# Attention feeding an MLP on one core: the last 64 tokens of every batch move to the final chunk, and the opening is re-ordered

## The chip, the cores and the metric

One core of a Trainium2 chip. The metric is device microseconds of one execution, taken as the median of the runs. One execution was also profiled, and its trace carries all line numbers (L...) used here. They are lines of the kernel before, unless the text says "of the changed kernel".

## The reference

Linear attention over 8 batches, 8 heads, 576 tokens and 64 dimensions, then an MLP with tanh shrinkage over the 4608 tokens:

```
phi(x) = where(x > 0, x, exp(x) - 1) + 1
kv  = einsum('bhsd,bhse->bhde', phi(k), v);   z = sum_s phi(k)
num = einsum('bhsd,bhde->bhse', phi(q), kv);  den = einsum('bhsd,bhd->bhs', phi(q), z) + 1e-6
x   = (num / den), transposed to (4608 tokens, 512)
h   = x @ w_in (512x2048);  g = h - tanh(h);  out = g @ w_out (2048x512)
```

q, k, v and the weights come in fp32; the loads turn them into bf16.

## The kernel before

**Tiling.** The 576 tokens of a batch are split as (64 positions p, 9 steps j), token 9p + j. `xT` (128, 4 pairs of heads, 4608 tokens) is the MLP's input, transposed; the MLP runs over NC = 9 chunks of 512 columns of `xT`. In a chunk, the first layer is 64 matmuls of 512 columns (`l1mm`, L434; in chunk 0 the first four blocks are L701 with 256 columns), then tanh on ScalarE (L440, L445) and the subtraction on VectorE (L441, L446) into `gT`; the second layer is 64 matmuls of 512 columns (`l2mm`, L455), an eviction to `osb` (L466) and stores (L479). Columns of `xT` lie batch after batch, 576 each, so chunk c needs batch c and the end of batch c - 1.

**Attention beside it.** The work of batch c + 1 and c + 2 is hung into the loops of chunk c: `s1[fi]` holds what is issued after block fi of the first layer, `s2[s]` what is issued after step s of the second. The order of every engine's instructions is the order in which the program issues them (manual schedule). Each engine works its own list in order and waits on semaphores.

**Names.** `phi_pieces` (L125) makes exp on ScalarE, max/add and min on VectorE. `a_qT_pe` (L161) transposes phi(q) on TensorE, nine blocks for each of two values of i, and copies them out of PSUM. `kv_mm` (L179) multiplies phi(k) by v, 72 matmuls of 64x64. For batch 0 it is `b0_kv` (64 columns), with the sums z apart in `b0_z` (L253). For batch 1 it is `a_kv`, whose right side is v next to a block of ones: 128 columns. For the others it is `kv_cols_mm`, with a packed copy `vp` of v that holds two columns of ones: 66 columns. `num_mm` (L274) makes the numerator of steps j = 0 to 7 (512 tokens), `rest_mm` (L282) that of j = 8 (64 tokens: "the rest"). `a_den` (L340) makes the denominators, L350 their reciprocal. In batches 0 and 1 the reciprocals of the first 512 tokens are spread over the partitions by TensorE (L303, L423) and those of the rest by a round trip through DRAM (`spread_rest`, L316 and L319), and the rest is scaled by `scale_rest` (L327).

**PSUM.** `ps_all` is 8 banks of 512 fp32 columns. The chunk loops use banks 0 to 5, the attention work of chunk 1 onward banks 6 and 7, besides banks 0 to 3 for the numerators (`a_num`, L378). `a_num` of the last batch (b = 7), issued in chunk 6, ends with copies of the numerators (banks 0 to 3) and of the rest (bank 6 by VectorE, bank 7 by ScalarE) into `xT`.

**Opening.** q, k and v of batch 0 arrive by GpSimd's DMA queue, then w_in, and behind a gate (`load_rest`) the other weights and batch 1. Dummy matmuls (`spin`, L542) fill TensorE's waits. The order on TensorE is: z of i = 0, z of i = 1, kv of i = 0, denominators, numerators, kv of i = 1, spread, L701.

Of the kernel before, what the change touches and what calls it, by code (L numbers as in the profile page):

```python
# [18 lines left out]
def kernel(  # L19
# [9 lines left out]
    nc = tc.nc  # L29
# [46 lines left out]
    kz_c = [const.tile([128, 2, 2, 96], BF16, name=f"kz{i}") for i in range(2)]  # L76

    v_b = [const.tile([128, 3, 2, J, D], BF16, name=f"v{i}") for i in range(2)]
# [4 lines left out]

    def load(b, t, src, halves):

        x = src[b].rearrange("h (p j) d -> (h p) (j d)", j=J)
        if halves:
            y = x.rearrange("(h i q) x -> i q h x", h=2, i=2)
            for i in range(2):
                for hs in ((0, 1), (1, 2)) if i and src is k and b == 0 else ((0, 2),):  # L90
                    nc.gpsimd.dma_start(out=t[:, hs[0]:hs[1], i].rearrange("q h j d -> q h (j d)"),
                                        in_=y[i, :, hs[0]:hs[1]])
        else:
            nc.gpsimd.dma_start(out=t.rearrange("q h i j d -> q (h i) (j d)"),  # L94
                                in_=x.rearrange("(n q) x -> q n x", n=4))
# [9 lines left out]
    def load_v(b):  # L105
        load(b, v_b[b % 2][:, 0:2], v, b < 2)
# [11 lines left out]
    def load_wo2(n):  # L118
        nc.gpsimd.dma_start(out=w_out_sb[:, 8 + 2 * n:10 + 2 * n, :],
                            in_=moe_w_out[1024 + 256 * n:1280 + 256 * n, :].rearrange("(ko ki) f -> ki ko f", ki=128))  # L120
# [4 lines left out]
    def phi_pieces(b, src, store, name, i, parts=0):  # L125
# [3 lines left out]
        x = src[b][:, :, i]  # L129
        e = epool.tile([128, 2, J, D], BF16, name="e")  # L130
        r = r_t[b] = epool.tile([128, 2, J, D], BF16, name="r")
        y = store[b][:, i].rearrange("p j h d -> p h j d")
        if parts:

            return ([lambda h=h: nc.scalar.activation(e[:, h], x[:, h], AF.Exp) for h in range(2)],  # L135
                    lambda: nc.vector.tensor_scalar(r, x, 0.0, 1.0, ALU.max, ALU.add),
                    [lambda h=h: nc.vector.tensor_tensor(y[:, h], e[:, h], r[:, h], ALU.min) for h in range(2)])
# [23 lines left out]
    def a_qT_pe(b, i, banks, on="AV"):  # L161
# [3 lines left out]
        for n in range(2):  # L165
            j0, j1 = ((0, 5), (5, 9))[n]
# [21 lines left out]
    def a_kv(b, b0):  # L188

        kz_t[b], vt = kz_c[b % 2], v_b[b % 2]  # L190
        kv_mm(b, lambda rs, h, i, j: vt[rs, h:3:2 - h, i, j, :],
              lambda cs, hg, i: ps_all[cs, b0 + hg, 128 * i:128 * i + 128].rearrange("p (a e) -> p a e", a=2))

    def a_kz(b, b0):
        ps = ps_all[:, b0:b0 + 2, 0:256].rearrange("p g (i e) -> p g i e", i=2)
        nc.vector.tensor_mul(kz_t[b][:, :, :, 64:96], ps[:, :, :, 64:96], mask)
        nc.vector.tensor_copy(kz_t[b][:, :, :, 0:64], ps[:, :, :, 0:64])

    def a_vp(b, i, eng=nc.vector):
        eng.tensor_copy(vp[:, i, :, :, 0:64].rearrange("p j h d -> p h j d"), v_b[b % 2][:, 0:2, i])  # L200

    def kv_cols_mm(b, b0, o):
        kz_t[b] = kz_c[b % 2]
        kv_mm(b, lambda rs, h, i, j: vp[rs, i, j, h, :],
              lambda cs, hg, i: ps_all[cs, b0 + hg, o + 66 * i:o + 66 * i + 66])
# [44 lines left out]
    def b0_z(i):  # L250

        for j in range(J):
            nc.tensor.matmul(ps_all[:, 5 - 3 * i, 0:2], kp_t[0][:, i, j].rearrange("p h d -> p (h d)"), two,  # L253
                             start=(j == 0), stop=(j == J - 1))

    def b0_zc(i):
        nc.vector.tensor_mul(kz_t[0][:, :, i, 64:96],
                             ps_all[:, 5 - 3 * i, 0:2].unsqueeze(2).to_broadcast([128, 2, 32]), mask[:, :, i, :])
# [18 lines left out]
    def rest_mm(b, b0, o):  # L277

        kz, qT = kz_t[b], qT_t[b]
        for i in range(2):  # L280
            for rs, cs, h, hg in quads():
                nc.tensor.matmul(ps_all[cs, b0 + h, 64 * i + o:64 * i + o + 64], kz[rs, hg, i, 0:64],  # L282
                                 qT[rs, i, 8, hg, :], start=True, stop=True)
# [28 lines left out]
    def spread_rest(b):  # L312

        ds = dram.tile([H, 4, 16], F32, name="ds0")
        for t in range(4):
            nc.sync.dma_start(out=ds[:, t, :], in_=rden_t[b][32 * t:32 * t + H, 128:144])  # L316
        rdb = rpool.tile([128, NP, 4, 16], F32, name="rdb0")
        for hh in range(2):
            nc.sync.dma_start(  # L319
                out=rdb[64 * hh:64 * hh + 64].rearrange("p a t c -> p (a t c)"),  # L320
                in_=ds[4 * hh:4 * hh + 4].rearrange("h t c -> (h t c)").partition_broadcast(64))
        rdb_t[b] = rdb

    def scale_rest(b, pss):
        rdb = rdb_t[b]
        for h, ps in enumerate(pss):
            nc.vector.tensor_mul(  # L327
                xT[:, 2 * h:2 * h + 2, S * b + 512:S * b + 576].rearrange("p a (t c) -> p a t c", t=4),
                ps.rearrange("p a (t c) -> p a t c", t=4), rdb[:, 2 * h:2 * h + 2])

    def a_den(b, bank, parts=range(4)):

        kz, qT = kz_t[b], qT_t[b]
        ps = ps_all[:, bank, 0:J * 16]
        for t in range(4) if b == 0 else ():
            nc.tensor.matmul(ps[32 * t:32 * t + 32], eps[:, 0:32], one[:, 0:J * 16], start=True, stop=False)
        for n, p in enumerate((0, 2, 1, 3)):
            if n in parts:
                for t in range(4):
                    nc.tensor.matmul(ps[32 * t:32 * t + 32], kz[:, p // 2, p % 2, 64:96],  # L340
                                     qT[:, p % 2, :, p // 2, 16 * t:16 * t + 16],
                                     start=(n == 0 and b > 0), stop=(n == NP - 1))
        if b > 0:
            den = rpool.tile([128, J * 16], F32, name="den")
# [3 lines left out]
        rden = rpool.tile([128, J * 16], F32, name="rden")  # L348
        for x in (slice(0, 128), slice(128, 144)) if b == 0 else (slice(0, 144),):
            nc.vector.reciprocal(rden[:, x], den[:, x])  # L350
        rden_t[b] = rden

    def a_split(b):

        f = rden_t[b]
        t1 = rpool.tile([128, J * 16], BF16, name="t1")
        u = rpool.tile([128, J * 16], F32, name="u")
        t2 = rpool.tile([128, J * 16], BF16, name="t2")
        w = rpool.tile([128, J * 16], BF16, name="w")
# [18 lines left out]
    def a_num(b, nxt):  # L378
# [8 lines left out]
        if b == B - 1:  # L387
            t = S * b + 448
            for h, copy in enumerate((nc.vector.tensor_copy, nc.scalar.copy)):
                two = slice(2 * h, 2 * h + 2)  # L390
                copy(xT[:, two, S * b:t], ps_all[:, two, 0:448])
                copy(xT[:, two, t:t + 128:2], ps_all[:, two, 448:512])
                copy(xT[:, two, t + 1:t + 128:2], rest[h])
        elif b >= QS:
            for h, copy in enumerate((nc.vector.tensor_copy, nc.scalar.copy)):
                copy(xT[:, 2 * h:2 * h + 2, S * b:S * b + 512], ps_all[:, 2 * h:2 * h + 2, :])
                copy(xT[:, 2 * h:2 * h + 2, S * b + 512:S * b + 576], rest[h])
# [3 lines left out]
    def num_scale(b, rest):  # L401

        rdb = rdb_t[b]
        for n in range(NP):
            nc.vector.tensor_mul(
                xT[:, n, S * b:S * b + 512].rearrange("p (j t c) -> p j t c", j=8, t=4),
                ps_all[:, n, :].rearrange("p (j t c) -> p j t c", j=8, t=4),
                rdb[:, n, :, 0:8, :].rearrange("p t j c -> p j t c"))
        for h in range(2):
            nc.vector.tensor_mul(  # L410
                xT[:, 2 * h:2 * h + 2, S * b + 512:S * b + 576].rearrange("p a (t c) -> p a t c", t=4),
# [14 lines left out]
    def a_scale(b, p, ns, n):  # L426
        nc.vector.tensor_mul(
            xT[:, p, S * b:S * b + 512].rearrange("p (j t c) -> p t j c", j=8, t=4),
# [31 lines left out]
    def evac(c, i, o, f0=0, f1=None):  # L460
# [7 lines left out]
        if c == NC - 1 and i == 3:  # L468
            nc.sync.dma_start(
                out=out[(B - 1) * S:, f0:f1].rearrange("(p j) m -> p j m", j=J)[:, J - 2:J],  # L470
# [3 lines left out]
        def store():  # L474
            for half in range(2):
                b, j = divmod(2 * (4 * c + i) + half, J)
                cuts = [f0, 256, f1] if c == 3 else [f0, f1]
# [21 lines left out]
    def load_rest(r):  # L499
        nc.gpsimd.tensor_copy(rpool.tile([1, 1], BF16, name="g0"), r[0:1, 1, J - 1, 63:64])  # L500
# [6 lines left out]
        load_wo2(0)  # L507
        nc.gpsimd.memset(v_b[1][:, 2], 1.0)
        nc.gpsimd.memset(vp[:, :, :, :, 64:66], 1.0)
        load_v(1)  # L510
        load_wo2(1)
        load_wo(3)
# [36 lines left out]
    spin(18)  # L549
    t0a, t0v = a_qT_pe(0, 0, side, "AA")  # L550
    t0a()
    (ek0, rk0, mk0), (ek1, rk1, mk1) = (phi_pieces(0, k_t, kp_t, "kp", i, 2 * i) for i in range(2))
    for f in (ek0, rk0):
        f()
    spin(4)
    t1a, t1v = a_qT_pe(0, 1, side)
    for f in (*ek1, t0v, t1a, mk0, rk1, *mk1):
        f()
    load_rest(r_t[0])
    spin(6)  # L560
# [4 lines left out]
    b0_z(1)  # L565
    b0_kv(0)
    b0_kz(0)
    b0_zc(1)
    a_den(0, 4)
# [5 lines left out]
    spread_rest(0)  # L575
# [21 lines left out]

    for c in range(NC):
# [4 lines left out]
        if c == 0:  # L603
# [7 lines left out]
            def kv1():  # L611
                a_kv(1, 4)
                pss = rest_mm(0, 4, 256)
                a_kz(1, 4)
                scale_rest(0, pss)
# [11 lines left out]
            s2[5].append(lambda: ([f() for i in range(2) for f in a_qT_pe(1, i, Banks([4 + 2 * i, 5 + 2 * i]))], a_kphi(1, 1),  # L627
# [3 lines left out]
            s2[10].append(lambda: (a_den(1, 4), num1(), spread_rest(1), a_split(1)))  # L631
# [16 lines left out]
            s2[13].append(lambda: exp2(qs, q_t, qp_t, "qp", 0))  # L648
            s2[14].append(lambda: exp2(qs, q_t, qp_t, "qp", 1))
            s2[15].append(lambda: (rest2(qs[0]), rest2(qs[1]), a_qT_dma(2), [f() for f in later], k2(0), k2(1)))  # L650
        elif n1 < B:
            if c == 1:
                def kv2():
                    kv_cols_mm(2, 6, 0)
                    pss = rest_mm(1, 6, 256)
                    kz_copy(2, 6, 0)
                    scale_rest(1, pss)
# [12 lines left out]
            s2[m].append(lambda: a_num(n1, n2 if n2 < B else 0))  # L670
            if n2 < B:
                s2[m + 2].append(lambda: (q_zb(n2, 4 if c == 1 else 7), q_prod(n2)))
                if c > 1:
                    s2[15].append(lambda: (q_den(n2, 0, 0), q_den(n2, 0, 1)))
        if c == 1:
# [53 lines left out]
        for s in range(16):  # L729
# [14 lines left out]
            if c == 0 and g == 2:  # L744
                for n in (2 * i, 2 * i + 1):
                    f = 8 + 2 * (n // 4)
# [37 lines left out]
```

## Time and profile before

| what | value |
|---|---|
| median of 3 runs | 284.19 us (284.14 to 284.21) |
| the profiled execution | 284.06 us |
| its span (first to last instruction) | 282.3 us |
| granted TensorE clock | 0.999 |
| TensorE busy | 274.2 us, 97% of the span |
| start of the first MLP matmul (L701) | 16.19 us |
| first 512-column matmul of the MLP (L434) | 20.01 us |
| last eviction (L464) | 279.15 us |

The span is what the trace covers; 1.8 us of the execution lie outside it. A duration of a matmul in the trace is its latency (379 ns for 512 columns), while matmuls that follow each other start about 216 ns apart (47 of them take 10.31 us in the chain of waits); so distances between starts are read, not durations.

### The profile page before, as it was taken

Reading aid. Unit: us, or ns where it says so; the run is one execution under the profiler, and the core shown is the slowest. Engines: PE = TensorE matmul, PEld = TensorE weight load, DVE = VectorE, ACT = ScalarE, POOL = GpSimd, SP = SyncE. Lnnn points to the kernel's source line nnn. Section 1 sums busy time; section 2 is a strip of 40 time slices with the busy share of each in tenths; the row PEclk is TensorE's granted clock in tenths of the full one; section 3 lists DMA queues with packets and bytes.
Section 4 is the critical chain, followed back from the end, with each engine's and each line's share of the span. In section 5 each row is a group of like instructions: output and inputs, shape, how many; then the busy total and the mean of one; then the engine's idle time right before and its main releaser. Section 6 shows DMA issues by size and latency. Waiting matters only on the chain.

```text
span 282.3 us, 5058 instructions
## 1 busy us (share of the span) xinstructions
PE 274.2 (97%) x2052; PEld 131.6 (47%) x2082; DVE 175.0 (62%) x281; ACT 145.9 (52%) x176; POOL 78.2 (28%) x71
## 2 busy tenths in 40 slices
PE   8899999999999999999999999999999999999995
PEld 3574464444444454445444544454444444444443
DVE  5759967994879764978397639764870167006600
ACT  3747648846356753566366735572651365126411
POOL 8663120330361526233614360506050000000000
PEclk9999999999999999999999999999999999999999
DMA  6999999899993399049903792252115210230032
GB/s 105 201 204 213 206 206 208 159 189 225 236 237 67 76 190 205 17 84 160 228 17 77 115 237 60 51 107 52 25 25 123 57 29 2 59 80 11 2 74 75
DMA packets 38759, 33.12 MB, mean 117 GB/s; under 512 B 16176, under 2 KB 34640, under 8 KB 38608
## 3 DMA queue, kind: packets, MB, share of 16 engines
q0 software_dynamic: 17520, 18.35, 40.2%
q1 hardware_dynamic: 21216, 14.45, 21.7%
q8 instruction: 16, 0.26, 0.3%
q14 instruction: 7, 0.06, 0.1%
HBM read 38.14 MB, written 9.46 MB: 169 GB/s over the span
## 4 chain that ended last, share of the span: by engine, by line
PE 90%; DMA 4%; ACT 2%; issue 2%; DVE 1%; SPq 0%; POOL 0%; DVEq 0%; POOLq 0%
PE ps_all L434 43%; PE ps_all L455 40%; DMA out_dram<-osb 2%; PE ps_all L185 2%; DMA qraw<-in_q_dram 2%; PE ps_all L701 1%; PE ps_all L274 1%; ACT osb L466 1%; ACT e L138 1%; SPq L479 0%; ACT e L135 0%; PE ps_all L303 0%; PE ps_all L340 0%; DVE rden L350 0%; ACT qT L173 0%
## 5 line engine op out<-in xcount | busy, mean ns | idle before, releaser
L455 PE MATMUL ps_all<-w_out_sb,gT 128*128 128x512 bf16 x542 | 122.6, 379 | 1.6 <-issue 1.0
L434 PE MATMUL ps_all<-xT,w_in_sb 128*128 128x512 bf16 x549 | 121.9, 379 | 0.7 <-issue 0.2
L441 DVE TENSOR_TENSOR gT<-ps_all,th 128x1024 bf16<-128x1024 f32 x64 | 77.8, 1218 | 45.9 <-ACT th L440 45.9
L440 ACT ACTIVATE th<-ps_all 128x1024 f32<-128x1024 f32 x64 | 65.5, 1023 | 47.4 <-PE ps_all L434 46.7
L434 PEld LDWEIGHTS <-w_in_sb 128*128 128x128 bf16 x560 | 54.7, 98 | 65.6 <-issue 0.3
L455 PEld LDWEIGHTS <-gT 128*128 128x128 bf16 x560 | 53.8, 98 | 63.1 <-issue 0.2
L466 ACT COPY osb<-ps_all 128x512 f32<-128x512 f32 (+1 forms) x36 | 20.9, 582 | 57.0 <-PE ps_all L455 39.3
L246 POOL TENSOR_TENSOR qp<-qp,rd 128x1152 bf16<-128x1152 bf16 x10 | 21.0, 2118 | 39.1 <-issue 23.7
L232 POOL TENSOR_TENSOR pr<-qp,zb 128x1152 f32<-128x1152 bf16 x10 | 23.4, 2360 | 21.0 <-ACT zb L225 18.5
L237 DVE TENSOR_REDUCE dn<-pr 128x9 f32<-128x576 f32 x20 | 14.5, 745 | 12.2 <-POOL pr L232 12.2
L138 ACT ACTIVATE e<-qraw 128x1152 bf16<-128x1152 bf16 x16 | 18.5, 1161 | 3.5 <-DMA qraw<-in_q_dram 3.5
L138 ACT ACTIVATE e<-kraw 128x1152 bf16<-128x1152 bf16 x15 | 17.4, 1162 | 2.1 <-DMA kraw<-in_k_dram 2.1
L140 DVE TENSOR_TENSOR qp<-e,r 128x1152 bf16<-128x1152 bf16 x16 | 12.1, 758 | 4.6 <-ACT e L138 3.6
L140 DVE TENSOR_TENSOR kp<-e,r 128x1152 bf16<-128x1152 bf16 x15 | 11.4, 757 | 5.0 <-ACT e L138 4.3
L94 POOL DMA_DIRECT2D kraw<-in_k_dram x7 | 5.5, 779 | 31.8 <-ACT e L138 31.8
L542 PE MATMUL ps_all<-zero 128*128 128x512 bf16 x29 | 9.0, 464 | 1.3 <-DVE zero L489 1.2
L94 POOL DMA_DIRECT2D qraw<-in_q_dram x7 | 5.2, 749 | 15.4 <-DVE r L139 8.2
L446 DVE TENSOR_TENSOR gT<-ps_all,th 128x512 bf16<-128x512 f32 x12 | 7.9, 688 | 0.9 <-ACT th L445 0.2
L445 ACT ACTIVATE th<-ps_all 128x512 f32<-128x512 f32 x12 | 7.2, 597 | 2.3 <-DVE gT L707 1.0
L200 DVE COPY vp<-v 128x1152 bf16<-128x1152 bf16 x10 | 5.2, 524 | 3.9 <-DMA v<-in_v_dram 3.9
L139 DVE TENSOR_SCALAR r<-qraw 128x1152 bf16<-128x1152 bf16 x16 | 7.3, 454 | 0.5 <-DMA qraw<-in_q_dram 0.5
L464 DVE COPY osb<-ps_all 128x128 f32<-128x128 f32 x1 | 0.3, 291 | 11.6 <-DMA out_dram<-osb 11.6
(108 smaller groups left out, 146.0 us busy)
## 6 DMA issues: line engine op xcount, KB each, us to landing
out_dram<-osb SPq DMA_DIRECT2D x62, 128.0 KB, 2.6
qraw<-in_q_dram POOLq DMA_DIRECT2D x7, 576.0 KB, 10.3
kraw<-in_k_dram POOLq DMA_DIRECT2D x7, 576.0 KB, 7.3
v<-in_v_dram POOLq DMA_DIRECT2D x6, 576.0 KB, 12.3
w_in_sb<-in_moe_w_in_dram POOLq DMA_DIRECT2D x3, 512.0 KB, 9.5
w_out_sb<-in_moe_w_out_dram POOLq DMA_DIRECT2D x3, 512.0 KB, 16.4
v<-in_v_dram POOLq DMA_DIRECT2D x4, 288.0 KB, 12.2
rdb<-ds SPq DMA_DIRECT2D x2, 576.0 KB
```

The costliest lines, as they stand in the source:

```text
L94: nc.gpsimd.dma_start(out=t.rearrange("q h i j d -> q (h i) (j d)"), in_=x.rearrange("(n q) x -> q n x", n=4))
L138: return (lambda: nc.scalar.activation(e, x, AF.Exp), lambda: nc.vector.tensor_scalar(r, x, 0.0, 1.0, ALU.max, ALU.add), lambda: nc.vector ...
L140: lambda: nc.vector.tensor_tensor(y, e, r, ALU.min))
L232: nc.gpsimd.tensor_mul(pr_t[b][:, i].rearrange("p j h d -> p j (h d)"), qp_t[b][:, i].rearrange("p j h d -> p j (h d)"), zb_t[b][:, i].uns ...
L237: nc.vector.tensor_reduce(dn_t[b][:, i, :, h], pr_t[b][:, i, :, h, :], mybir.AxisListType.X, ALU.add)
L246: nc.gpsimd.tensor_mul(x, x, rd[:, i].unsqueeze(2).to_broadcast([128, J * 2, D]))
L434: nc.tensor.matmul(h, w_in_sb[:, p, fi * 128:(fi + 1) * 128], xT[:, p, c * 512:(c + 1) * 512], start=(n == 0), stop=(n == NP - 1))
L440: nc.scalar.activation(th, h, AF.Tanh)
L441: nc.vector.tensor_sub(gT[:, fi:fi + 2, :], h, th)
L455: nc.tensor.matmul(o, gT[:, fi, i * 128:(i + 1) * 128], w_out_sb[:, fi, :], start=(fi == 0), stop=(fi == NF - 1))
L466: nc.scalar.copy(osb[:, f0:f1], o[:, f0:f1])
L542: nc.tensor.matmul(ps_all[:, 0, :], zero[:, 0:128], zero, start=True, stop=True)
```

## The change

Seven parts.

1. Columns of `xT`: batch b's first 512 tokens (j = 0 to 7) are now chunk b, and the 64 tokens with j = 8 of all batches make up chunk 8. Stores follow this.
2. q of batches 0 and 1 is loaded without j = 8, so its phi, its transposes (eight blocks, not nine) and its denominators (128 columns, not 144) are smaller. `spread_rest` and `scale_rest` go away, and so do the `rest_mm` of batch 0 (in chunk 0) and of batch 1 (in chunk 1).
3. The 64 tokens of these two batches take a path of their own: `load_qr` (four DMAs on GpSimd's queue in chunk 4), `r_phi` (chunk 6: exp, max/add, min on 512 columns and a transpose by SyncE's queue), `r_den` and `r_num` (chunk 6, right behind `a_num` of batch 7; banks 6 and 7), a round trip of their reciprocals through DRAM on SyncE's queue, and `r_scale` (four multiplications on VectorE in chunk 7).
4. kv of batch 1 uses the packed `vp` (66 columns). The copies into `vp` are on VectorE (i = 0, and h = 0 of i = 1) and ScalarE (h = 1 of i = 1).
5. Opening: k of batch 0 is loaded in four quarters and its phi is worked by quarters; z uses banks 3 and 2 (5 and 2 before); z of i = 1, its scaling and the denominators come ahead of kv of i = 0; three dummy matmuls fewer; the gate of `load_rest` hangs on the end of phi(k).
6. Chunk 0: the second half of w_out arrives in pieces of 2, 1, 1, 2, 2 blocks (2, 2, 4 before), and the second layer's steps 8 to 15 take the blocks in that order (`plan0`).
7. Four buffers for kz (two before). The exps of q of batch 2 are issued one step later. In chunk 3 three of the stores are not cut in two.

```
-    kz_c = [... for i in range(2)]
+    kz_c = [... for i in range(4)]
+    def main(b):            # steps j in the main part
+        return J - 1 if b < 2 else J
+    def rest_at(b):         # place of the rest in xT
+        return 512 * B + 64 * b
+    def load_qr():
+        for b in range(2):
+            for i in range(2):
+                nc.gpsimd.dma_start(out=qr[:, b, i], in_=q[b].rearrange(
+                    "(h i g) (p j) d -> i (g p) h j d", h=2, i=2, j=J)[i, :, :, J - 1])
-            j0, j1 = ((0, 5), (5, 9))[n]
+            j0, j1 = 4 * n, 4 * n + 4
+    def r_phi():            # exp, max/add, min on [128, 512], then
+        nc.sync.dma_start_transpose(out=qT_t["r"]..., in_=y)
+    def r_den(bank, o):
+        ps = ps_all[0:64, bank, o:o + 64]
+        ...                 # 8 matmuls of 64 columns
+        nc.vector.tensor_scalar(den, ps, 1e-6, None, ALU.add)
+        nc.vector.reciprocal(rden, den)
+        ...                 # 2 + 4 DMAs on SyncE: to DRAM and back, broadcast
+    def r_num(b0, o):
+        pr_t["r"] = [rest_mm(b, b0, o + 128 * b, qT_t["r"][:, b].unsqueeze(2)) for b in range(2)]
+    def r_scale():
+        for b in range(2):
+            for h, ps in enumerate(pr_t["r"][b]):
+                nc.vector.tensor_mul(xT[:, 2 * h:2 * h + 2, rest_at(b):rest_at(b) + 64], ps, ...)
 opening
-    spin(18)
+    spin(17)
-    (ek0, rk0, mk0), (ek1, rk1, mk1) = (phi_pieces(0, k_t, kp_t, "kp", i, 2 * i) for i in range(2))
+    (ek0, rk0, mk0), (ek1, rk1, mk1) = (phi_pieces(0, k_t, kp_t, "kp", i, 1) for i in range(2))
-    for f in (*ek1, t0v, t1a, mk0, rk1, *mk1):
+    for f in (*ek0, *ek1, t0v, t1a, *rk0, rk1[0], *mk0, rk1[1], *mk1):
-    spin(6)
+    spin(4)
     b0_z(0); spin(2); b0_zc(0); t1v(); b0_z(1)
+    b0_zc(1)
+    a_den(0, 4)
     b0_kv(0); b0_kz(0)
-    b0_zc(1)
-    a_den(0, 4)
     b0_num(0); b0_evac(0, ns0); b0_kv(1); b0_kz(1)
-    spread_rest(0)
 chunk 0
-                a_kv(1, 4)
-                pss = rest_mm(0, 4, 256)
-                a_kz(1, 4)
-                scale_rest(0, pss)
+                kv_cols_mm(1, 4, 0)
+                kz_copy(1, 4, 0)
 chunk 1
                     kv_cols_mm(2, 6, 0)
-                    pss = rest_mm(1, 6, 256)
                     kz_copy(2, 6, 0)
-                    scale_rest(1, pss)
 chunks 4, 6 and 7
+            if c == B - 4:
+                s2[m + 1].append(load_qr)
+            if c == B - 2:
+                s1[9].append(r_phi)
+                s2[m].append(lambda: (r_den(7, 384), r_num(6, 128)))
+        if c == B - 1:
+            s1[3].append(r_scale)
```

## The prediction

> **What bounds the kernel now.** I read the page's first and fourth parts, the chain of waits in order of time, then the timelines of TensorE, ScalarE and VectorE at the places that the diff touches.
>
> From the page, busy shares by engine, then shares of the chain by engine:
>
> ```profile
> PE 274.2 (97%) x2052; PEld 131.6 (47%) x2082; DVE 175.0 (62%) x281; ACT 145.9 (52%) x176; POOL 78.2 (28%) x71
> ...
> PE 90%; DMA 4%; ACT 2%; issue 2%; DVE 1%; SPq 0%; POOL 0%; DVEq 0%; POOLq 0%
> ```
>
> TensorE is the bound. From 20 us on it runs its list almost without a hole, so what is taken out of its list, or put in as a wait, is the change in time. Ahead of 16 us it waits for others.
>
> From the chain (start, length, engine, line):
>
> ```profile
> 11.37 0.36 PE ps_all L253 x9
> ...
> 13.28 1.08 DVE rden L350 x2
> ...
> 14.40 1.22 PE ps_all L303 x32
> ...
> 16.19 3.77 PE ps_all L701 x32
> ...
> 39.95 1.13 PE ps_all L185 x72
> 41.08 0.06 PE ps_all L282 x8
> ...
> 57.86 0.71 PE ps_all L185 x72
> 58.57 0.22 PE ps_all L282 x8
> ...
> 75.52 0.62 PE ps_all L185 x72
> 76.14 0.16 issue
> ```
>
> The reader sees the opening's order, the wide kv of batch 1 with a rest behind it (39.95), the packed kv of batch 2 with batch 1's rest (57.86), and a packed kv without a rest behind it (75.52), which is what both become.
>
> From ScalarE's timeline: the opening, then the rest copies of chunk 5 and the numerator copy of chunk 6.
>
> ```profile
> 9.60 1.24 ACT L135 ACTIVATE e<-kraw 128x576 bf16<-128x576 bf16 x2
> 10.75 1.16 ACT L173 COPY qT<-ps_all 128x512 bf16<-128x512 bf16 x2
> ...
> 190.98 0.27 ACT L397 CAST xT<-ps_all 128x128 bf16<-128x128 f32 x1 [0.53 <-DVE kz L215]
> ...
> 218.55 0.91 ACT L391 CAST xT<-ps_all 128x896 bf16<-128x896 f32 x1 [1.74 <-PE ps_all L282]
> ```
>
> **The change part by part**, against the profiled execution of 284.06 us.
>
> Opening. q of batch 0 is a ninth smaller; ScalarE starts its second exp when the second half lands, 6.90 before and about 6.64 after. Then ScalarE is back to back: exp 0.95 (1.07 start to start, less a ninth), a copy of 512 columns 0.47, four exps of 576 columns at 0.575 each: the last ends at 10.45 (10.84 before). VectorE's min per quarter takes 0.42, so phi(k) ends at 10.96 (11.80 before) and z of i = 1 starts at 11.0 (12.03 before). Behind it on VectorE stand the first scaling of z 0.23, a copy 0.41 and the second scaling 0.22, ending near 11.85. The denominators take TensorE from 11.87 to 12.25 (16 matmuls, 12.80 to 13.18 before). The reciprocal, now one of 128 columns at 0.96, ends at 13.26; before, the spread waited for both, until 14.36. But ahead of the spread TensorE now has kv of i = 0 (0.41, to 12.66), ScalarE's copy of it (0.14 to its start, 0.27, to 13.07), the numerators (0.24 from 13.11) and kv of i = 1 (0.41 from 13.35). So the spread starts at 13.79, not 14.40: gain 0.61. The steps behind it keep their 1.79 to L701. What would hide more: the second piece of w_in landed at 15.59, is earlier by q's ninth (0.26), and is needed at about 16. Bounds: 0.35 (quarters of k that come late by one exp's half) and 1.1 (the reciprocal alone sets the spread). I take 0.6.
>
> Quarters of k: in the trace the two quarters that exist, issued 0.55 apart, landed 5.0 us after issue, as a half did after 4.9, so an extra issue costs GpSimd 0.56, with transfers still queued behind: nothing.
> The Trainium skill ("DMA: Bandwidth & Descriptors") puts about 2 us of fixed cost on each DMA and asks for large ones. In series that would be 2 us more for the split and an estimate near 287. The rows show the fixed part overlapped.
>
> Transposes of batch 1: 18 took 1.00 us in chunk 0, 16 take 0.89: gain 0.11.
>
> kv of batch 1: 72 matmuls of 128 columns and 8 of the rest, 39.95 to 41.14, are 1.19. A packed kv alone is 0.78 (0.62 and 0.16, the row at 75.52): gain 0.39, bounds 0.25 (0.94 at worst, the row at 131.12 with 0.77 and 0.16) and 0.45. I take 0.37. Denominators of 128 columns instead of 144, and no longer a wait of 0.4 in two for VectorE's rest scaling: 0.08. The copies into vp have a cost: v of batch 1 landed at 39.30, and now ScalarE's copy (0.57 for 576 columns) stands between it and kv, while TensorE comes there 0.7 us earlier. v itself comes earlier by q's ninths (0.26 each for two batches) and the missing round trip of 128 KB (0.3), so at about 38.5, and kv may start at 39.1 to 39.2, when TensorE is there: cost 0.05, bounds 0 and 0.35.
>
> kv of batch 2 without batch 1's rest: 57.86 to 58.95 is 1.09, becomes 0.78: gain 0.31, bounds 0.2 and 0.45. I take 0.30.
>
> Sum of the gains: 0.61 + 0.11 + 0.37 + 0.08 + 0.30 - 0.05 = 1.42.
>
> Chunk 6 is the cost. `r_den` writes columns 384 to 447 of bank 7 and `r_num` columns 128 to 383 of banks 6 and 7, right behind `a_num` of batch 7, whose rest lies in columns 0 to 127 of both. The trace shows that waits go by bank: at 190.98 ScalarE's copy of columns 0 to 127 of bank 7 waited 0.53 us for VectorE's kz copy, which reads columns from 128 on. So `r_den` waits for ScalarE's copies of batch 7: from 218.55, 1.01 for 1024 columns (as its copy of that size at 189.44; the row of 896 above took 0.91), 0.27 for the rest less 0.10 overlap, ends 219.73; `r_den` starts at 219.79 and its eight matmuls end, with latency, at 220.08. `r_num`'s second half of each quad is bank 7 and waits for VectorE's add on the denominators (0.20, as the rows of L345 at 0.3 for 144 columns suggest, to 220.33); bank 6 is free by then (VectorE's copies 1.22 + 0.28 from 218.52). `r_num`'s 16 matmuls take 0.20, and the second layer, queued behind on TensorE (L455, which came back at 218.53), comes back at 220.63: cost 2.10. Bounds: 0.30 (matmuls alone, if columns decided) and 2.4 (a slower copy and each release 0.1 more). I take 2.10, by the row at 190.98. Nobody else needs r_num early; that the steps behind wait is the whole price. A stall cannot be made up later, as TensorE has no holes.
> The Trainium skill ("PSUM — Partial Sum Buffer", "PSUM bank collisions raise a hardware error") says that two engines may not touch one bank in the same 32 partitions, whatever the columns, and asks to guard by bank. It speaks against putting these steps here; guarded by columns the execution would be 282.9.
>
> At nothing: `load_qr` puts four issues of about 0.75 on GpSimd in chunk 4 (161.5 to 164.5) ahead of `pr` (L232, 163.8), which slips 0.7; the denominators behind it on VectorE have 1.4 to the next L441 (0.7 lost if that is wrong). `r_phi`'s exp (0.6) lies in ScalarE's gaps of 0.70 between tanh, its 0.25 and 0.4 in VectorE's of 0.50. SyncE's queue gets one transpose behind that of batch 7 (209.7, 2.45) and six small DMAs ahead of chunk 6's later stores: `osb` has five buffers, a store issue waits, no engine. Reciprocals are back at 226 to 229, `r_scale` (four of 0.28 on VectorE, near 232) is needed at 253. w_out's pieces land at 39.1, 40, 41.3 and 42.6 and are needed at 39.7, 41.5, 43 and 44. Without that cover one step waits, 0.3.
>
> 284.06 - 1.42 + 2.10 = 284.74. The median of the runs is 0.13 above the profiled execution: 284.87, so 284.9. Its own range is 284.5 to 285.2.
>
> **The rivals.** A difference of 0.2%, 0.57 us, is about what a measurement of this kernel can tell from no change (283.62 to 284.76).
>
> Opening set by the reciprocal (not slower). If kv, its copy and the numerators fit beside the reciprocal, by v being there and ScalarE idle from 11 us, the spread starts at 13.3, gain 1.1, and the time is 284.4. It decides once the opening gains 0.72. For it: in the trace the spread waited 0.50 on the reciprocal and nothing else. Against it: kv and numerators are then not ahead of it but all before it, and take 1.54 in my sum. Chance 0.27.
>
> Gains that are not there (slower still). Short groups of 64x64 matmuls are followed by a hole of 0.16 in the chain at 76.14 and by less at 41.08; with 0.35 in the opening, 0.25 and 0.2 for the two kv and 0.35 lost on the copy of v, all gains are 0.64: 285.65. For it: v's landing at 39.30 against kv at 39.95. Chance 0.16.
>
> The stall isn't there. If `r_den` and `r_num` do not wait, cost 0.30: 283.1. Against it: the row at 190.98 and that the changed program holds these waits. Chance 0.06.
>
> Round trip late: if the reciprocals come back after VectorE reaches `r_scale` (232), VectorE waits in front of the subtractions, and the second layer waits too; an estimate is 286.2, for 1.3 us of wait. Against it: more than 3 us lie between 229 and 232. Chance 0.06.
>
> **How the numbers follow.** My sum has 0.45: of this 0.30 is slower and 0.15 within 0.2%. Slower: 0.30 + 0.16 + 0.06 = 0.52. Within: 0.15 + 0.24 of the first rival = 0.39. Faster: 0.03 of the first rival + 0.06 = 0.09. The range 284.2 to 285.7 leaves out the missing stall, the late round trip and the first rival's best end, 0.03 to 0.06 each.
>
> **What would show it.** In the changed profile: L701 at 15.6; the kv of batch 1 at 0.78 without a row of the rest behind it, and whether ScalarE's copy of v precedes it at once; 58 us likewise; at 217 to 219 us the second layer standing for 2.1 us, first on ScalarE's copy of the rest, then on VectorE's add. I am wrong if that stop is under 1 us, or L701 starts before 15.2 or after 15.9.

## The result, and the profile after

The changed kernel takes 287.45 us (286.62 to 289.72, six runs) against 284.20 (284.07 to 284.23): a ratio of 1.0128, interval 1.0091 to 1.0165. It is slower by 3.25 between the medians and 3.6 by the ratio, where 0.7 was forecast, and its own runs lie 3 us apart. Two of its six runs, 288.58 and 289.72, had a granted TensorE clock of 0.994, the other four 1.000. Its profiled execution is one of the four and takes 287.70, span 285.9.

The page, engines and then shares of the chain:

```profile
PE 273.7 (96%) x2053; PEld 130.8 (46%) x2083; DVE 179.3 (63%) x288; ACT 146.5 (51%) x178; POOL 80.8 (28%) x77
...
PE 82%; DMA 7%; DVE 4%; issue 2%; ACT 1%; POOL 1%; SPq 0%; DVEq 0%; POOLq 0%
```

TensorE is busy as long as before. But the chain has lost 8 points of TensorE, to DMA (4 before) and VectorE (1 before). Who made TensorE wait is in the waits of TensorE (total, times, longest):

```profile
PE ps_all L485 <- DVE gT L471: 1.9, 1, 1.9
PE ps_all L341 <- ACT xT L427: 1.2, 1, 1.2
...
PE ps_all L464 <- DMA w_in_sb<-in_moe_w_in_dram: 0.9, 1, 0.9
```

Three single waits, and none of the three stood in the profile before. The second is `r_den`, as forecast. The first and the third were not.

The first wait, in the timeline of chunk 6, all engines:

```profile
205.16 4.24 POOL L257 TENSOR_TENSOR qp<-qp,rd 128x1152 bf16<-128x1152 bf16 x2 [7.89 <-issue]
...
206.04 1.39 DVE L330 TENSOR_SCALAR r<-qr 128x512 bf16<-128x512 bf16 x1
...
207.53 2.15 DVE L331 TENSOR_TENSOR qpr<-e,r 128x512 bf16<-128x512 bf16 x1
...
209.61 3.58 DVE L471 TENSOR_TENSOR gT<-ps_all,th 128x1024 bf16<-128x1024 f32 x3
210.87 2.32 PE L485 MATMUL ps_all<-w_out_sb,gT 128*128 128x512 bf16 x10 [1.89 <-DVE gT L471]
```

The same place in the kernel before:

```profile
205.46 4.19 POOL L246 TENSOR_TENSOR qp<-qp,rd 128x1152 bf16<-128x1152 bf16 x2 [7.89 <-issue]
...
206.92 1.23 DVE L441 TENSOR_TENSOR gT<-ps_all,th 128x1024 bf16<-128x1024 f32 x1 [0.50 <-ACT th L440]
...
208.65 1.22 DVE L441 TENSOR_TENSOR gT<-ps_all,th 128x1024 bf16<-128x1024 f32 x1 [0.50 <-ACT th L440]
...
209.12 3.19 PE L455 MATMUL ps_all<-w_out_sb,gT 128*128 128x512 bf16 x13
```

`r_phi`'s two steps on VectorE take 1.39 and 2.15 us, where 0.25 and 0.4 were counted. GpSimd's two multiplications of q of batch 7 (2.12 and 2.17) run beside them, and VectorE's two steps end 0.15 and 0.29 after them. In the kernel before the same multiplications run beside VectorE's subtractions, which keep their 1.22. The subtraction L471 stands behind them in VectorE's list, and TensorE's second layer needs it. The distance between two neighbouring 512-column matmuls here is 2.05 us over the usual 0.216.

The second, TensorE's timeline at the end of `a_num`, before and then after:

```profile
217.85 0.63 PE L274 MATMUL ps_all<-qT,kz 64*64 64x512 bf16 x8
218.30 0.23 PE L282 MATMUL ps_all<-qT,kz 64*64 64x64 bf16 x8
218.47 5.35 PE L455 MATMUL ps_all<-w_out_sb,gT 128*128 128x512 bf16 x23
```

```profile
220.05 0.23 PE L294 MATMUL ps_all<-qT,kz 64*64 64x64 bf16 x8
221.53 0.29 PE L341 MATMUL ps_all<-qTr,kz 128*32 128x64 bf16 x8 [1.25 <-ACT xT L427]
...
222.20 0.32 PE L294 MATMUL ps_all<-qTr,kz 64*64 64x64 bf16 x15 [0.23 <-DVE denr L344]
222.68 1.67 PE L485 MATMUL ps_all<-w_out_sb,gT 128*128 128x512 bf16 x7 [0.16 <-issue]
```

The order of waits is the one forecast: ScalarE's copy of the rest, VectorE's add, then the second layer. The stop is 3.17 us over the usual distance, 0.71 before: 2.46.

The third, TensorE's timeline of the opening:

```profile
15.79 3.77 PE L749 MATMUL ps_all<-xT,w_in_sb 128*128 128x256 bf16 x32 [0.27 <-DVE xT L319]
20.43 0.81 PE L464 MATMUL ps_all<-xT,w_in_sb 128*128 128x512 bf16 x3 [0.88 <-DMA w_in_sb<-in_moe_w_in_dram]
```

The first MLP matmul starts 0.40 earlier (16.19 before), and the first of 512 columns 0.42 later (20.01): the gain is waited away for the third piece of w_in.

Bookkeeping of the two profiled executions, as distances between neighbouring 512-column matmuls less 0.216, after minus before:

| place | before | after | difference | predicted |
|---|---|---|---|---|
| start of the first 512-column matmul | 20.01 | 20.43 | +0.42 | -0.61 |
| transposes of batch 1 | 1.00 | 0.89 | -0.11 | -0.11 |
| kv of batch 1 | 1.29 | 0.96 | -0.33 | -0.37, and +0.05 for v |
| denominators and numerators of batch 1 | 1.34 | 1.24 | -0.10 | -0.08 |
| kv of batch 2 | 1.25 | 1.03 | -0.22 | -0.30 |
| chunk 6, `r_phi` | 0 | 2.05 | +2.05 | 0 |
| chunk 6, `r_den` and `r_num` | 0.71 | 3.17 | +2.46 | +2.10 |
| last eviction to the end | 2.85 | 2.51 | -0.34 | 0 |
| sum | | | +3.83 | +0.68 |

The executions differ by 3.64; 0.2 is not placed.

### The profile page after: what moved, and what is told of

It is laid out like the page before. It is cut to its first block, busy times and chain, and to the rows that moved or that the text cites. A ratio compares the mean times of both kernels' runs of the same rounds, so it can differ in the third digit from the quotient of the medians.

```text
span 285.9 us, 5068 instructions
## 1 busy us (share of the span) xinstructions
PE 273.7 (96%) x2053; PEld 130.8 (46%) x2083; DVE 179.3 (63%) x288; ACT 146.5 (51%) x178; POOL 80.8 (28%) x77
## 4 chain that ended last, share of the span: by engine, by line
PE 82%; DMA 7%; DVE 4%; issue 2%; ACT 1%; POOL 1%; SPq 0%; DVEq 0%; POOLq 0%
PE ps_all L485 40%; PE ps_all L464 39%; DMA w_in_sb<-in_moe_w_in_dram 3%; DMA out_dram<-osb 2%; DMA kraw<-in_k_dram 2%; PE ps_all L204 2%; DVE gT L471 2%; PE ps_all L285 1%; DVE qpr L331 1%; ACT osb L496 1%; SPq L509 0%; DVE r L330 0%; DVE dn L248 0%; POOL qraw L101 0%; POOL kraw L101 0%
## 5 line engine op out<-in xcount | busy, mean ns | idle before, releaser
L464 PE MATMUL ps_all<-xT,w_in_sb 128*128 128x512 bf16 x550 | 122.0, 379 | 1.5 <-DMA w_in_sb<-in_moe_w_in_dram 0.9
L471 DVE TENSOR_TENSOR gT<-ps_all,th 128x1024 bf16<-128x1024 f32 x64 | 77.5, 1217 | 44.4 <-ACT th L470 44.4
L464 PEld LDWEIGHTS <-w_in_sb 128*128 128x128 bf16 x560 | 54.6, 98 | 66.6 <-DMA w_in_sb<-in_moe_w_in_dram 0.9
L157 ACT ACTIVATE e<-qraw 128x1152 bf16<-128x1152 bf16 (+1 forms) x16 | 18.0, 1134 | 3.3 <-DMA qraw<-in_q_dram 3.2
L157 ACT ACTIVATE e<-kraw 128x1152 bf16<-128x1152 bf16 x14 | 16.3, 1162 | 2.5 <-DMA kraw<-in_k_dram 2.5
L159 DVE TENSOR_TENSOR qp<-e,r 128x1152 bf16<-128x1152 bf16 (+1 forms) x16 | 11.9, 742 | 4.3 <-ACT e L157 3.3
L159 DVE TENSOR_TENSOR kp<-e,r 128x1152 bf16<-128x1152 bf16 x14 | 10.8, 772 | 4.5 <-ACT e L157 3.9
L426 DVE CAST xT<-ps_all 128x1024 bf16<-128x1024 f32 x5 | 6.1, 1216 | 7.1 <-PE ps_all L294 7.1
```

The costliest lines, as they stand in the source:

```text
L157: return (lambda: nc.scalar.activation(e, x, AF.Exp), lambda: nc.vector.tensor_scalar(r, x, 0.0, 1.0, ALU.max, ALU.add), lambda: nc.vector ...
L159: lambda: nc.vector.tensor_tensor(y, e, r, ALU.min))
L464: nc.tensor.matmul(h, w_in_sb[:, p, fi * 128:(fi + 1) * 128], xT[:, p, c * 512:(c + 1) * 512], start=(n == 0), stop=(n == NP - 1))
L471: nc.vector.tensor_sub(gT[:, fi:fi + 2, :], h, th)
```

## The experiments

Kernels were run in three groups, each beside the kernel before; ratios are to that one, and compare better than microseconds across groups.

**1. `r_phi` behind block 1 of chunk 6 instead of block 9.**

```
-                s1[9].append(r_phi)
+                s1[1].append(r_phi)
```

> Only r_phi moves, from behind block 9 to behind block 1 of chunk 6's first layer, where GpSimd runs nothing (197.3 to 205.2 us in the changed kernel's trace). Theory (VectorE's two steps of r_phi, 1.39 and 2.15 us, waited for GpSimd's two long multiplications of q of batch 7, and the subtractions behind them stopped TensorE for 2.05 us at 208.5): the steps take about 0.25 to 0.3 and 0.4 us, TensorE's stop is gone, 287.45 - 2.05 = 285.4. Rival (the two steps are slow by themselves, from their tiles or shapes): they keep 1.4 and 2.1 us, the stop moves to about 200 us, 287.4. If the scatter of the changed kernel's runs (286.6 to 289.7) comes from this place, it falls below 0.5.

Measured: 285.61 us, ratio 1.0040 (1.0019 to 1.0061); the changed kernel had 1.0128. That is 2.5 us less, 2.05 was expected. If only the runs with a granted clock of 0.998 or more are taken, the medians lie 2.92 (changed kernel) and 0.87 above the kernel before beside them, which makes 2.05. These runs spread over 1.1 us in both kernels (286.6 to 287.7, and 284.7 to 285.8), so the scatter does not come from this place.

**2. The gate of `load_rest` back on VectorE's last max/add of k.**

```
-        nc.gpsimd.tensor_copy(g0, kp_t[0][0:1, 1, J - 1, 1, 63:64])
+        nc.gpsimd.tensor_copy(g0, r[0:1, 1, J - 1, 63:64])     # r = r_t[0]
```

> Only the gate of load_rest moves back, from the end of phi(k) to VectorE's last max/add of k (some 0.75 us earlier). Theory (the third piece of w_in is issued behind the gate, at 11.82 where it was 11.16 before, and its landing at 20.16 sets the first 512-column matmul at 20.43): issue near 11.1, first 512-column matmul at 19.7 or 19.8, 287.45 - 0.67 = 286.8. Rival (the landing is set by the bytes queued ahead of it, not by the issue): it lands at 20.1 all the same, 287.4.

Measured: 288.09, ratio 1.0131 (1.0080 to 1.0182): nothing to be seen. In its profile the third quarter of k came so late that w_in's third piece was issued at 11.77, as late as in the changed kernel (11.82), and L749 started only at 16.42; w_in's third piece was not waited for. This run cannot tell what the gate is worth.

**3. `r_den` and `r_num` three and four steps later.**

```
-                s2[m].append(lambda: (r_den(7, 384), r_num(6, 128)))
+                s2[m + 3].append(lambda: r_den(7, 384))
+                s2[m + 4].append(lambda: r_num(6, 128))
```

> Only r_den and r_num move: from right behind a_num of batch 7 to three and four steps of the second layer later (2.6 and 3.5 us), when the copies out of banks 6 and 7 are done. Theory (the stop at 219.2 us, 3.17 us long where the kernel before has 0.71, is the wait for these copies and for VectorE's add): what is left is the 24 small matmuls, about 0.3, so 287.45 - 2.15 = 285.3. Rival (the small matmuls and their weights themselves cost it, or the stop only moves): 287.0 to 287.5.

Measured: 286.04, ratio 1.0063 (1.0034 to 1.0092), about 1.9 less than the changed kernel. The distance behind `a_num` is 0.71 again, as in the kernel before, and the moved groups leave 0.32 and 0.34: 0.66 where 0.3 was expected. The stop was the wait for the copies, and it did not reappear elsewhere. TensorE's timeline, with L341 for `r_den` and the last L294 for `r_num`:

```profile
220.01 0.23 PE L294 MATMUL ps_all<-qT,kz 64*64 64x64 bf16 x8
220.17 2.76 PE L485 MATMUL ps_all<-w_out_sb,gT 128*128 128x512 bf16 x12
222.86 0.29 PE L341 MATMUL ps_all<-qTr,kz 128*32 128x64 bf16 x8
223.09 1.04 PE L485 MATMUL ps_all<-w_out_sb,gT 128*128 128x512 bf16 x4
224.06 0.32 PE L294 MATMUL ps_all<-qTr,kz 64*64 64x64 bf16 x16
```

**4. All three moves.**

> The three moves together (r_phi behind block 1, gate on the max/add, r_den and r_num three and four steps later). Theory (three separate losses, additive): 287.45 - 2.05 - 0.67 - 2.15 = 282.6, faster than the kernel before by 1.6. Rival (they share a cover, as when one stop gives time to another): 283.5 to 284.5.

Measured: 283.00, ratio 0.9948 (0.9931 to 0.9966), five runs of 282.7 to 283.6. `r_phi` in its profile, VectorE's timeline:

```profile
198.00 0.28 DVE L330 TENSOR_SCALAR r<-qr 128x512 bf16<-128x512 bf16 x1
198.39 0.43 DVE L331 TENSOR_TENSOR qpr<-e,r 128x512 bf16<-128x512 bf16 x1
```

The same two steps take 0.28 and 0.43 where GpSimd runs nothing. They are not slow by themselves. None of the three waits above is in this profile, and the change, without them, is faster than the kernel before. By the ratios this is 5.1 below the changed kernel, where the three losses together were put at 4.87.

**5. and 6. The wait by itself, in the kernel before.** Nothing of the change is in it but two steps of `r_phi`'s kind, behind block 9 and behind block 1.

```
+            if c == B - 2:
+                def probe():
+                    nc.vector.tensor_scalar(r, xT[:, 0, 0:512], 0.0, 1.0, ALU.max, ALU.add)
+                    nc.vector.tensor_tensor(y, xT[:, 1, 0:512], r, ALU.min)
+                s1[9].append(probe)        # the other kernel: s1[1]
```

> The kernel before with two VectorE steps added in chunk 6 behind block 9 of the first layer: max/add and min on 512 bf16 columns, SBUF to SBUF, the shapes of r_phi, into tiles that nobody reads. Nothing else of the change. Theory (they wait for GpSimd's two multiplications of q of batch 7, 205.5 to 209.7 us): 1.4 and 2.1 us long, each ending 0.1 to 0.3 behind one of GpSimd's, TensorE stops for about 2.0, 284.2 + 2.0 = 286.2. Rival (the steps are slow only in the changed kernel): 0.25 and 0.4 us, 284.2.

> The same two added steps behind block 1, where GpSimd runs nothing. Theory: 0.25 and 0.4 us, no stop, 284.2. Rival (VectorE has no room for 0.65 us in this chunk wherever it is put): a stop of 0.1 to 0.5 near 200 us, 284.3 to 284.7.

Measured behind block 9: 286.18, ratio 1.0074 (1.0061 to 1.0087): 2.1 us. Behind block 1: 284.23, ratio 1.0001 (0.9992 to 1.0009): nothing. VectorE's timeline behind block 9, GpSimd's in the same stretch, and VectorE's behind block 1:

```profile
206.20 1.39 DVE L674 TENSOR_SCALAR pbr<-xT 128x512 bf16<-128x512 bf16 x1
207.63 2.22 DVE L675 TENSOR_TENSOR pby<-xT,pbr 128x512 bf16<-128x512 bf16 x1
```

```profile
205.33 4.24 POOL L246 TENSOR_TENSOR qp<-qp,rd 128x1152 bf16<-128x1152 bf16 x2 [7.89 <-issue]
```

```profile
199.57 0.28 DVE L674 TENSOR_SCALAR pbr<-xT 128x512 bf16<-128x512 bf16 x1
199.89 0.42 DVE L675 TENSOR_TENSOR pby<-xT,pbr 128x512 bf16<-128x512 bf16 x1
```

Behind block 9 it is the changed kernel's picture with other data and other tiles. Place beside GpSimd decides, and two steps of 0.7 us in all cost 2.1.

**7. One step with a fp32 result in the same place.**

```
+                    nc.vector.tensor_scalar(r, xT[:, 0, 0:512], 0.0, 1.0, ALU.max, ALU.add)   # r in fp32
+                s1[9].append(probe)
```

> The kernel before with one VectorE step behind block 9 of chunk 6: max/add of 512 columns, bf16 in, fp32 out, nothing else added. Theory (only the steps of 16-bit data or of two SBUF operands wait for GpSimd; in the trace of before VectorE's reductions of fp32 run beside GpSimd at their usual 0.74): about 0.6 us, no stop over 0.3, 284.2 to 284.4. Rival (every SBUF to SBUF step of VectorE waits): 1.4 us as with bf16, a stop of about 0.5, 284.7.

Measured: 284.17, ratio 0.9988 (0.9968 to 1.0009), so no time is lost, but VectorE's timeline shows that the step waited:

```profile
206.17 1.52 DVE L674 TENSOR_SCALAR pbr<-xT 128x512 f32<-128x512 bf16 x1
```

My account was too narrow: a fp32 result does not spare the step. And one wait of this kind is hidden by VectorE's slack, while the two in a row of the probe before cost 2.1.

**8. The two stops removed, the changed kernel's own gate kept.**

> The changed kernel with r_phi behind block 1 and r_den and r_num later, and its own gate of load_rest (the end of phi(k)). Against the kernel with all three moves (283.0, 0.9948 of the kernel before) this tells what the gate is worth. Theory (the third piece of w_in is issued 0.67 later and lands that much later): 283.0 + 0.67 = 283.7, with a TensorE wait on w_in at 19 to 23 us. Rival (the queue's bytes set the landing): 283.0. The kernel with the gate alone moved gave 1.0131 against 1.0128 for the changed kernel, with intervals of 0.005 and 0.004, which tells neither.

Measured: 283.94, ratio 1.0005 (0.9980 to 1.0029), runs from 283.1 to 287.0. With the gate moved as well the first group gave 0.9948, and the last group 0.9972 (0.9949 to 0.9996). The second pair of intervals overlaps, so what the gate costs in the median is not settled. What the profiles show: w_in's third issue at 11.80 let TensorE go on without a wait here, as it landed 7.45 later, and at 11.82 in the changed kernel, with a landing 8.34 later, cost it 0.88.

**9. kv of i = 0 ahead of the denominators again, with the three moves.**

```
+    b0_kv(0); b0_kz(0)
     b0_zc(1)
     a_den(0, 4)
-    b0_kv(0); b0_kz(0)
```

> The kernel with all three moves, and in the opening kv of i = 0 and its copy again ahead of the second scaling of z and the denominators, as in the kernel before; k still in quarters. Theory (the reciprocal, 0.96, then ends after kv and numerators, and the spread waits for it): the reciprocal starts about 0.45 later, the spread 0.3 to 0.5 later, 283.0 + 0.4 = 283.4. Rival (what gained was the 16-column reciprocal that went and the smaller q, not the order): 283.0.

Measured: 283.70, ratio 0.9986 (0.9974 to 0.9998). Its profile contradicts the theory: from the start of z of i = 1 to the spread it takes 2.24 us with this order, 2.43 with the changed order (in all profiles that have it but that of the first experiment, where the clock fell and it took 2.88) and 2.38 in the kernel before. Its L749 starts at 15.59, 0.05 later than with three moves, though its z of i = 1 starts 0.24 later. What its execution loses (0.77 to the other profile) lies mostly elsewhere: two waits of 0.26 and 0.33 at 77 to 79 us, where the reciprocals of batch 2 came back late. The new order of the opening gains nothing.

**10. to 12. The last group.**

```
 three again: as number 4
 k in three:  -  ((0, 1), (1, 2)) if src is k and b == 0 else
              +  ((0, 1), (1, 2)) if i and src is k and b == 0 else
 best:        +  s2[m + 3].append(lambda: (r_num(6, 128), r_den(7, 384)))
              and kv of i = 0 ahead of the denominators
```

> The kernel with the three moves once more (r_phi behind block 1, gate on VectorE's last max/add of k, r_den and r_num later), beside the two that follow. Expected as the first time: 283.0, 0.995 of the kernel before, scatter under 1 us.

> The three moves, and k of batch 0 loaded in three DMAs as before (i = 0 whole, i = 1 in halves), its phi still by quarters. Theory (the third quarter's landing, 9.3 to 10.2 us in the profiles so far, holds ScalarE's exp and so z; a fourth DMA only adds to the queue): z of i = 0 waits for the whole half, z of i = 1 as early as before, within 0.2 of the kernel with three moves. Rival (splitting the first half is what brought phi(k) forward): 0.4 later.

> The three moves, with two more: r_num and r_den together in one step of the second layer, r_num first, so that TensorE waits for no add of VectorE; and kv of i = 0 ahead of the denominators, as in the kernel before. From the traces: one hole less among the 512-column matmuls (0.3 each), and from z of i = 1 to the spread 2.24 us with that order where the changed order has 2.43. Theory: 283.0 - 0.2 - 0.2 = 282.6. Rival (the order of the opening costs elsewhere, as the 283.7 of the run with that order alone may say): 283.0 to 283.5.

Measured: 283.47, 0.9972 (0.9949 to 0.9996), scatter 283.0 to 286.4 where under 1 us was expected; 283.39, 0.9968 (0.9949 to 0.9987); 283.23, 0.9967 (0.9946 to 0.9989). All three beat the kernel before by 0.8 to 1.0 and cannot be told from each other. The k loads in four pieces gain nothing over three. `r_num` ahead of `r_den` leaves one distance of 0.57 instead of 0.32 and 0.34, so 0.1 and not 0.2.

## Why the prediction was wrong

The sign was right, the size was a fifth of what came. Step by step:

- **At nothing, `r_phi`.** This is the step that failed. I named as cover the gaps of VectorE and ScalarE and did not ask what GpSimd ran in them. Cost: 2.05 in the trace, 2.1 in the probe, 2.5 in the kernel with `r_phi` moved. The trace before could have told it: none of the 72 steps of VectorE on bf16 data from SBUF to SBUF (L139, L140, L200) lay beside one of GpSimd's multiplications, while 9 of the 20 reductions (L237) and 16 of the 64 subtractions (L441) did, at their usual 0.74 and 1.22. The Trainium skill states it ("SBUF — State Buffer", section "Who interferes with whom"): VectorE and GpSimd share a pair of ports, held for a whole instruction by the one that comes first, and a copy or scalar step in one of the modes that use both ports, or a step with two operands in SBUF, waits for GpSimd's to end; reductions do not. The three probes agree: 1.39 and 2.22 beside GpSimd, 1.52 there with a fp32 result, 0.28 and 0.42 where GpSimd runs nothing. No run moved GpSimd's multiplications and left the steps in place.
- **Opening, 0.61.** L749 came 0.40 earlier, not 0.61: phi(k) ended at 11.53, not 10.96, as the third quarter of k landed at 9.49 and ScalarE waited 0.29 for it. In other profiles of this opening it cost ScalarE up to 0.77, and the fourth up to 1.01. The spread started at 14.01, where the sum has 13.79. Then the term turned into a loss. I had read that the gate of `load_rest` hangs on phi(k) now, and counted the landing of w_in's second piece only. The third is issued behind the gate, 0.66 later than before, and landed at 20.16; L464 needed it at 19.5. From issue to landing it took 8.34, against 7.72 before and 7.0 to 8.5 in the other profiles, so the late gate and the slow landing share this wait. The first rival, the reciprocal that sets the spread, did not appear: in every profile of this order the spread follows kv of i = 1.
- **Chunk 6, 2.10.** Right in mechanism and order, and 0.36 too small. ScalarE's copies ended at 221.48, 1.18 after the numerators' 220.30; that took as long as counted. `r_den` to its add took 0.40 instead of 0.29, and behind the last wait TensorE had 0.16 more before its next full matmul, as behind every small group. The moved groups still cost 0.66, where the lower bound said 0.30.
- **The small gains** were within 0.1: transposes 0.11 (0.11), kv of batch 1 0.33 (0.37), denominators 0.10 (0.08), kv of batch 2 0.22 (0.30). In the sum's working for batch 1, 1.19 less 0.78 is 0.41, where it says 0.39; the 0.37 it took stands. ScalarE's copy of v ended at 40.61 and held TensorE up by 0.15 inside kv; in the third experiment's profile it and VectorE's copy cost about 0.55.
- **The other costs at nothing** (`load_qr`, SyncE's queue, the round trip, w_out in pieces) left no wait of TensorE in the profile.
- **Rivals.** The one with gains that are not there had the direction but another mechanism. The stall that isn't there is refuted by the profile and the third run. The round trip was in time: its last load was issued at 225.8 and landed 2.5 later, and `r_scale` ran at 233.55 without a wait.

The sum is 284.74 + 2.05 + 1.03 + 0.36 - 0.34 + 0.05 (the small gains and the 0.05 charged to v) = 287.89 with these terms right, against 287.70.

What stays open is the gate's share in the median, and why some runs are so much longer. What goes with them is on record: of the 92 runs of kernels with the new opening, 17 have a mean granted clock of 0.988 to 0.994, and in each kernel that has any they are the longest; every run of the kernel before and of the probes in the three groups has 0.998 or more. Two profiles caught such a run, the first experiment's (289.18) and that of the three moves again (286.41). In both, TensorE's clock is 0.50 for about 3.4 us in the opening, from 13.1 and from 14.7, and L464 starts at 21.01 and 21.31 (19.14 to 20.43 in the other profiles of this opening). The spread in the second of them, and in the changed kernel at clock 1.00:

```profile
14.55 1.96 PE L315 MATMUL ps_all<-rden,sel 32*128 32x128 f32 x32
```

```profile
14.01 1.17 PE L315 MATMUL ps_all<-rden,sel 32*128 32x128 f32 x32
```

The change takes three dummy matmuls out of the opening, and the prediction priced nothing for the clock. Whether they are the reason was not tested: TensorE stood idle for 0.83 and 1.06 us in one piece ahead of the fall, but for 1.19 in the second experiment's profile, where the clock stayed at 1.00. The profiled execution of the changed kernel has clock 1.000 throughout its opening, so none of this is in the sum above.

## What to carry to other kernels

When an instruction is put into a gap of one engine, look at what every other engine runs in that gap, not only at the width of the gap. Where two engines in a trace never overlap in one kind of step, ask whether that is chance before you place such a step beside the other. A group of small matmuls belongs behind the copies out of its PSUM banks: three and four steps of the stage later it cost 0.7 instead of 2.5.

## What the runs showed that I had not expected

- VectorE's steps on SBUF data (0.28 and 0.43 us) took 1.39 and 2.15 beside GpSimd's multiplications of 2.12 and 2.17, in the changed kernel and, as 1.39 and 2.22, in the kernel before with the two steps added. The second waited almost the whole of GpSimd's next instruction, which had begun before it.
- In the two profiles with the low clock the same happened once more, in chunk 1, with GpSimd's two copies of v. They ran beside VectorE's two max/adds, which took 2.72 us together in the first experiment and 1.77 in the three moves again, instead of 0.82, and TensorE stopped for 2.04 and 1.09. In the other profiles GpSimd starts its copies as these steps end, and there is no stop. From the first experiment:

```profile
51.41 2.91 POOL L208 COPY vp<-v 128x1152 bf16<-128x1152 bf16 x2 [10.05 <-DMA v<-in_v_dram]
...
51.92 2.72 DVE L158 TENSOR_SCALAR r<-kraw 128x1152 bf16<-128x1152 bf16 x2
...
55.82 1.46 PE L464 MATMUL ps_all<-xT,w_in_sb 128*128 128x512 bf16 x6 [1.87 <-DVE gT L471]
```

- The last store goes to two batches instead of two neighbouring tokens: its issue took 0.37 instead of 0.55, and the execution ended 2.51 after the last eviction instead of 2.85, and by 2.51 to 2.54 in the other profiles of the changed kernel. That is 0.34 of gain, which the sum did not have.
